# Attention followed by expert routing on one Trainium2 core: moving the token table to the last steps and loading four experts' weights ahead

## The chip, the cores and the metric

The kernel runs on one core of a Trainium2 chip, as one launch. The metric is the device time of the launch in microseconds, taken as the median of several runs. Beside it there is one profiled execution, with its own time, which the trace describes. Engine names in the profile are PE (TensorE matmul), PEld (its weight loads), DVE (VectorE), ACT (ScalarE), POOL (GpSimd) and SP (SyncE). POOL also issues most of the transfers.

## The reference: what is computed

First comes block-causal attention, for 8 batches of 8 heads with 576 positions and head size 64. A position sees all positions of its own 64-wide block and of the blocks before it. The result is laid out as x, 4608 rows (tokens) of 512. Then each row goes through the expert that `moe_domain_id` names for it, one of 8:

```
mask = block_i >= block_j
attn = exp(scores - max); attn = attn / (sum(attn) + 1e-09)
x = (attn @ v).transpose(0, 2, 1, 3).reshape(4608, 512)
for e in range(8):
    out[domain_id == e] = relu(x[domain_id == e] @ w1[e]) @ w2[e]
```

w1[e] is 512 x 1024 and w2[e] is 1024 x 512, both given in float32. The kernel computes in float16 with float32 sums.

## The kernel before

**Attention.** The work is cut into 32 pairs of heads, p = 0 to 31, four per batch. The loop at L445 runs 33 steps, the last of which only drains. In step p the program order is: scores of the first group for pair p (`emit_G(0)`, L323, then the exponential on ACT, L328); the transposes of q and k for pair p+2 (`emit_T`, L311 on PE, copied out of PSUM by DVE at L315); scores of the second group; the products with v for pair p-1 (`emit_P`, L374 and L379); scores of the third group; the rest of p-1 and its normalisation (`emit_Q`, L395 and L396 on DVE); then one piece of the table (L477); then `loads(p)` (L427). The transposes write into PSUM tiles of the tag PT, of which there are two; the table's sums use the same two.

**Loads.** q and k are loaded and cast to float16 on the way by POOL's queue (L69). v comes in float32 into one of three staging tiles `vst` (L78, L82) and is then cast by POOL into `vS` (L110, `cast_v`). Batch b is loaded at step 4b-10, so the last one, b = 7, at step 18, and its v is cast at step 20. In that same `loads(p)` a batch's loads enclose the cast of the batch before. POOL works through its instructions in the order of the program, so casts, table work, load issues and gathers stand in one queue.

**Weights.** An expert's weights are eight pieces, four of w1 (L116) and four of w2 (L119), each of 512 KB in float32 in memory and 256 KB in float16 on the chip. The eight pieces of experts 0 and 1 go into the pool `wsb` (two buffers of each kind), two pieces per step in steps 20 to 27. Experts 2 to 7 use four buffers in the pool `msb`, which is opened after the attention's pool `asb` is closed. Expert 2 is issued after the gathers of experts 0 and 1, expert e+3 during the second product of expert e.

**The table.** `inverse` (L169) turns the rank and domain of each token into a table of row numbers for each expert's 640 slots. It works on four quarters of the columns. For each quarter `differ` makes two differences on POOL (Hq at L184, L at L187), `equal` compares on DVE (L193, L195, L197), `column` multiplies on POOL (L204), and `add` sums with nine matmuls on PE (L213) and one DVE instruction (L217 or L219). Four short DVE instructions (L226 to L234) finish it. It is a generator. One `next` is made at the end of each step from p = 18 on, just before `loads(p)`:

```
for k in range(10):
    for d, f in ((3, add), (2, column), (1, equal), (0, differ)):
        if (k - d) % 2 == 0 and 0 <= k - d < 8:
            f((k - d) // 2)
    yield
```

So a quarter starts every second step, and each of its four stages comes one step after the one before. The first `add` stands at the end of step 21, the last at the end of step 27, and the finish at step 28.

**Between the two halves.** The rows x of a batch are stored to memory as they are done (L412 and L413, on SP's queue, the last part also on ACT's). After the loop 36 matmuls on the identity (L486) run on PE. Then POOL issues the gathers of expert 0 and 1 (L498, five blocks of 128 rows each), which need the table and all the stored rows.

**Experts.** For each expert the first product is `mm1` (L530, then the rectifier on ACT, L536) and the second is `mm2` (L547), whose result DVE copies (L553) and POOL scatters to the output (L554). Between the blocks of `mm2` PE transposes the next expert's rows (L508, copied by DVE at L511). Expert 0 alone does `mm1` in two halves, the first for blocks 0 to 2. A loop at L609 handles experts with more than 640 tokens.

Of the kernel before, what the change touches and what calls it, by code (L numbers as in the profile page):

```python
# [9 lines left out]
F32 = mybir.dt.float32  # L10
F16 = mybir.dt.float16
# [7 lines left out]
def kernel(  # L19
# [11 lines left out]
    B, H, S, D = q.shape  # L31
    N = B * S
    E = moe_w1.shape[0]
# [21 lines left out]

    qh = [asb.tile([128, HP, S], F16, name=f"qh{i}") for i in range(4)]
    kh = [asb.tile([128, HP, S], F16, name=f"kh{i}") for i in range(4)]
    vst = [asb.tile([128, 5, H, D], F32, name=f"vst{i}") for i in range(3)]


    vS = [asb.tile([128, 5, HP, 132], F16, name=f"vS{i}") for i in range(3)]
# [69 lines left out]
    def load_weights(pool, bufs, w1_e, w2_e):  # L131
        w1h, t1 = load_w1(pool, bufs, w1_e)
        w2h, t2 = load_w2(pool, bufs, w2_e)
        return w1h, w2h, t1 + t2


    ones_sq = const.tile([128, 128], F16, name="ones_sq")
    lo_h = const.tile([128, NJ], F16, name="lo_h")
    u_f = const.tile([128, NJ], F32, name="u_f")
# [29 lines left out]
    def inverse(sb, pp, tag, ncols, base, tok):  # L169
        ub = sb.tile([128, NJ], F16, name="ub", tag="ub")  # L170
        nc.vector.tensor_scalar(
            out=ub[:], in0=u_f[:], scalar1=base, scalar2=None, op0=ALU.subtract)
        inv = sb.tile([128, 2, ncols], F32, name="inv", tag="inv")
        fi = inv[:].rearrange("p a c -> p (a c)")
        sh, sl = [128, NQ, ncols], [128, NQ, 128]
        ts = {}

        def differ(qt):
            js = slice(NQ * qt, NQ * qt + NQ)
            L = sb.tile([128, NQ, 128], F16, name="L", tag="L", bufs=2)  # L180
            Hq = sb.tile([128, NQ, ncols], F16, name="Hq", tag="Hq", bufs=2)
            Hh = sb.tile([128, NQ, 2, ncols], F16, name="Hh", tag="Hh", bufs=2)
            ts[qt] = (L, Hq, Hh)
            nc.gpsimd.tensor_tensor(  # L184
                out=Hq[:], in0=iota_h[:, 0:ncols].unsqueeze(1).to_broadcast(sh),
                in1=ub[:, js].unsqueeze(2).to_broadcast(sh), op=ALU.subtract)
            nc.gpsimd.tensor_tensor(  # L187
                out=L[:], in0=iota_h[:].unsqueeze(1).to_broadcast(sl),
                in1=lo_h[:, js].unsqueeze(2).to_broadcast(sl), op=ALU.subtract)

        def equal(qt):
            L, Hq, Hh = ts[qt]
            nc.vector.tensor_scalar(  # L193
                out=Hq[:], in0=Hq[:], scalar1=0.0, scalar2=None, op0=ALU.is_equal)
            nc.vector.tensor_scalar(  # L195
                out=L[:], in0=L[:], scalar1=0.0, scalar2=None, op0=ALU.is_equal)
            nc.vector.tensor_scalar(  # L197
                out=Hh[:, :, 0], in0=Hq[:], scalar1=p_f[:, 0:1], scalar2=None,
                op0=ALU.mult)

        def column(qt):
            L, Hq, Hh = ts[qt]
            js = slice(NQ * qt, NQ * qt + NQ)
            nc.gpsimd.tensor_tensor(  # L204
                out=Hh[:, :, 1], in0=Hq[:],
                in1=iota_h[:, js].unsqueeze(2).to_broadcast(sh), op=ALU.mult)

        def add(qt):
            L, Hq, Hh = ts[qt]
            ps = pp.tile([128, 512], F32, name=tag, tag=tag, bufs=2)  # L210
            pv = ps[:, 0 : 2 * ncols]
            for j in range(NQ):
                nc.tensor.matmul(  # L213
                    out=pv, lhsT=L[:, j], rhs=Hh[:, j].rearrange("p a c -> p (a c)"),
                    start=(j == 0), stop=(j == NQ - 1))
            if qt == 0:
                nc.vector.tensor_copy(out=fi, in_=pv)  # L217
            else:
                nc.vector.tensor_tensor(out=fi, in0=fi, in1=pv, op=ALU.add)  # L219

        for k in range(10):
            for d, f in ((3, add), (2, column), (1, equal), (0, differ)):
                if (k - d) % 2 == 0 and 0 <= k - d < 8:
                    f((k - d) // 2)
            yield
        nc.vector.tensor_tensor(  # L226
            out=inv[:, 0], in0=inv[:, 0], in1=inv[:, 1], op=ALU.add)
        nc.vector.tensor_scalar(
            out=inv[:, 1], in0=inv[:, 0], scalar1=0.0, scalar2=1.0e6,
            op0=ALU.is_equal, op1=ALU.mult)  # L230
        nc.vector.scalar_tensor_tensor(
            out=tok[:, 0], in0=inv[:, 0], scalar=-4.0, in1=inv[:, 1],
            op0=ALU.add, op1=ALU.add)
        nc.vector.tensor_scalar(  # L234
            out=tok[:, 1], in0=tok[:, 0], scalar1=float(N - 1), scalar2=None,
            op0=ALU.min)
        yield
# [189 lines left out]
    def loads(p):  # L427
        fn = nc.gpsimd.tensor_copy
        for b in range(2, B):
            if p == max(0, 4 * b - 10):  # L430
                load_qk(b)
                load_v(nc.gpsimd, b, range(0, 5))
                cast_v(fn, b - 1)
                load_v(nc.gpsimd, b, range(5, H + 1))
        if p == 4 * B - 12:
            cast_v(fn, B - 1)
            for e in range(2):
                w1s[e], w2s[e], t = load_weights(wsb, 2, moe_w1[e], moe_w2[e])
                wts.extend(t)
        for f in wts[:2]:  # L440
            f()
        del wts[:2]

    prev = None
    for p in range(npair + 1):  # L445
        b, hp = divmod(p, HP)
        st = None
        if p < npair:
            st = {"p": p, "QK": QKs.pop(p)}
            if hp == 0:  # L450
                x_t = asb.tile([128, 6, DM], F16, name="x", tag="x", bufs=2)
            st["x"] = x_t
            emit_G(0, st)
        if p and p + 2 < npair:
            QKs[p + 2] = emit_T(p + 2)
        if p < npair:
            emit_G(1, st)
        if prev is not None:
            emit_P(prev)
        if p < npair:  # L460
            emit_G(2, st)
        if prev is not None:
            emit_Q(prev)
            if prev["p"] == npair - 2:
                store_x(prev, 0, DM - 128, nc.sync)
            elif prev["p"] == npair - 1:
                store_x(prev, DM - 128, DM, nc.scalar)
            elif prev["p"] % HP == HP - 1:
                store_x(prev, 0, DM, nc.sync)
        if p == 0:  # L470
            cast_v(nc.scalar.copy, 0)
            QKs[1] = emit_T(1)
            emit_VE(0)
            QKs[2] = emit_T(2)
        if p < npair and hp == 3 and b + 1 < B:
            emit_VE(b + 1)
        if p > 17:  # L477
            next(tabl, None)
        loads(p)
        prev = st  # L480
    for _ in tabl:
# [95 lines left out]
        nc.vector.memset(base_f[:], float(NB * E))  # L577

    xgs = {e: gather(tok_of(e)) for e in range(2)}
    w1s[2], w2s[2], todo = load_weights(msb, 4, moe_w1[2], moe_w2[2])  # L580
    for f in todo:
        f()
    xT = new_xT()
    for e in range(E):
        if e + 2 < E:
            xgs[e + 2] = gather(tok_of(e + 2))
        hT = new_hT()
        if e == 0:
            for i, blks in enumerate(((0, 1, 2), (3, 4))):
                for blk in blks:  # L590
                    transpose_block(xgs[0], xT, blk)
                mm1(xT, hT, w1s[0], (i,))
        else:
            mm1(xT, hT, w1s[e])
        nxt = None
        if e + 1 < E:
            xT = new_xT()
            nxt = (xgs[e + 1], xT)
        todo = ()
        if e + 3 < E:  # L600
            w1s[e + 3], w2s[e + 3], todo = load_weights(
                msb, 4, moe_w1[e + 3], moe_w2[e + 3])
        if e == 1:
            count_rounds()
        mm2(hT, w2s[e], tok_of(e), outs[NB * e : NB * e + NB], todo, nxt)
# [3 lines left out]
    with tc.For_i(0, n_it, 1) as it:  # L609
        e_r = it % E  # L610
        tok = msb.tile([128, 2, NB], I32, name="tok", tag="tok")
        for _ in inverse(msb, mps, "po", NB, base_f[:, 0:1], tok[:]):
            pass
        nc.vector.tensor_scalar(out=base_f[:], in0=base_f[:], scalar1=float(NB),
                                scalar2=None, op0=ALU.add)
        w1h, w2h, todo = load_weights(
            msb, 4, moe_w1[bass.ds(e_r, 1)].rearrange("o d f -> (o d) f"),
            moe_w2[bass.ds(e_r, 1)].rearrange("o d f -> (o d) f"))
        for f in todo:
            f()  # L620
        xg, xT, hT = gather(tok), new_xT(), new_hT()
        for blk in range(NB):
            transpose_block(xg, xT, blk)
        mm1(xT, hT, w1h)
        mm2(hT, w2h, tok, outs[0:NB])
# [30 lines left out]
```

## Time and profile before

| | us |
|---|---|
| median of 9 runs | 333.24 |
| lowest and highest | 330.51 and 336.85 |
| the profiled execution's own time | 336.27 |
| its span, first to last instruction | 334.6 |
| PE busy in the span | 273.9 |
| POOL busy | 220.6 |
| DVE busy | 148.0 |
| ACT busy | 146.3 |
| last PE instruction of the attention, end | 151.5 |
| first matmul of `mm1`, start | 163.3 |

The profile page gives busy times per engine, then the span in 40 slices with a digit for the busy tenths, the clock that TensorE was granted (PEclk) and the share of time in which the 16 DMA engines were busy, and then groups of instructions by line. The trace can be asked for the timeline of an engine, for who waited for whom, and for busy times in any stretch. A wait is written as the line that waited, an arrow and what ended the wait.

### The profile page before, as it was taken

To read this page: it belongs to the slowest core of one execution; us is meant where nothing else is said; L and a number is where in the kernel's file an instruction comes from. 1 tells how busy PE (TensorE), PEld (TensorE's weight loads), DVE (VectorE), ACT (ScalarE), POOL (GpSimd) and SP (SyncE) were. 2 spreads that over 40 slices of the span, in tenths; PEclk is the share of its full clock that TensorE was granted. 3 is DMA by queue.
4 is the path that set the end of the run, shared out by engine and by line. 5 is a ranking of instruction groups with operands and counts; after the bars stand their busy time and mean duration, and the time that the engine had idled before them with its cause. 6 is when DMAs were issued, how large, how long until landed. Compare 5 with 4: busy or idle time off the path is not lost. (4 is left out here: it accounts for less than half of the span.)

```text
span 334.6 us, 8598 instructions
## 1 busy us (share of the span) xinstructions
PE 273.9 (82%) x3658; PEld 177.3 (53%) x3658; DVE 148.0 (44%) x286; ACT 146.3 (44%) x208; POOL 220.6 (66%) x286
## 2 busy tenths in 40 slices
PE   2579887697972889869669999999899899999930
PEld 1357665465751567645335665647466464656510
DVE  3857887376782978651102514040230504042120
ACT  5549787386871568680232240505124060513300
POOL 8669968798899996002786868687786766223230
PEclk9999999597896789799979999999999999999995
DMA  8999999899969399722369998989899695212030
GB/s 161 201 208 200 178 234 202 191 202 227 265 103 265 59 176 211 147 72 80 102 131 246 181 252 170 223 199 216 224 191 235 137 226 174 78 39 104 31 115 1
DMA packets 36537, 55.69 MB, mean 166 GB/s; under 512 B 9902, under 2 KB 22702, under 8 KB 36496
## 3 DMA queue, kind: packets, MB, share of 16 engines
q0 software_dynamic: 26128, 49.17, 69.6%
q1 hardware_dynamic: 9840, 5.81, 6.2%
q8 instruction: 30, 0.49, 0.6%
q10 hardware_dynamic: 528, 0.13, 0.2%
q14 instruction: 11, 0.09, 0.1%
HBM read 67.15 MB, written 15.20 MB: 246 GB/s over the span
## 5 line engine op out<-in xcount | busy, mean ns | idle before, releaser
L328 ACT ACTIVATE A<-ps 128x1024 f16<-128x1024 f32 (+1 forms) x96 | 83.0, 883 | 46.8 <-PE ps L323 31.0
L536 ACT ACTIVATE hT<-ph 128x640 f16<-128x640 f32 (+1 forms) x72 | 46.4, 645 | 117.0 <-PE ph L530 111.2
L547 PE MATMUL po<-w2h,hT 128*128 128x512 f16 x320 | 74.9, 379 | 4.2 <-DVE osb L553 3.6
L530 PE MATMUL ph<-xT,w1h 128*128 128x320 f16 x512 | 73.3, 302 | 3.6 <-DVE xT L511 2.6
L554 POOL DMA_INDIRECT out_dram<-osb,tok x40 | 40.8, 1019 | 44.9 <-DVE osb L553 30.4
L498 POOL DMA_INDIRECT xg<-x_rows,tok x40 | 40.9, 1024 | 37.0 <-issue 36.4
L530 PEld LDWEIGHTS <-w1h 128*128 128x128 f16 x512 | 50.5, 99 | 26.1 <-issue 2.8
L511 DVE COPY xT<-pt 128x512 f16<-128x512 f16 x40 | 16.9, 424 | 105.9 <-PE pt L508 67.5
L78 POOL DMA_DIRECT2D vst<-in_v_dram x56 | 42.8, 796 | 14.0 <-DMA kh<-in_k_dram 7.8
L547 PEld LDWEIGHTS <-hT 128*128 128x128 f16 x320 | 30.1, 98 | 34.3 <-issue 5.0
L315 DVE COPY QK<-PT 128x576 f16<-128x576 f16 x64 | 45.5, 749 | 4.0 <-PE PT L311 3.7
L379 PE MATMUL po<-vS,A 128*128 128x65 f16 x640 | 37.2, 203 | 4.9 <-issue 4.9
L323 PE MATMUL ps<-QK 64*128 64x512 f16 (+3 forms) x256 | 37.8, 335 | 3.9 <-ACT A L328 2.3
L379 PEld LDWEIGHTS <-A 128*128 128x128 f16 x640 | 32.6, 104 | 6.8 <-issue 6.8
L553 DVE COPY osb<-po 128x512 f32<-128x512 f32 x40 | 27.4, 684 | 19.7 <-PE po L547 19.7
L374 PE MATMUL po<-VE,ATE 128*128 128x130 f16 x160 | 33.3, 234 | 2.5 <-DVE x L396 2.5
L396 DVE TENSOR_TENSOR x<-po,rc 128x768 f16<-128x768 f32 x32 | 30.6, 958 | 1.1
L311 PE MATMUL PT<-identh,kh 64*64 64x64 f16 x576 | 17.1, 203 | 8.5 <-DVE inv L219 2.8
L311 PE MATMUL PT<-identh,qh 64*64 64x64 f16 x576 | 17.2, 206 | 5.3 <-DVE QK L315 4.1
L374 PEld LDWEIGHTS <-ATE 128*128 128x128 f16 x160 | 16.0, 100 | 9.8 <-issue 7.5
L311 PEld LDWEIGHTS <-qh 64*64 64x64 f16 x576 | 13.8, 119 | 13.6 <-issue 12.6
L395 DVE RECIPROCAL rc<-po 128x12 f32<-128x12 f32 x32 | 7.4, 232 | 30.2 <-PE po L374 30.2
(85 smaller groups left out, 241.9 us busy)
## 6 DMA issues: line engine op xcount, KB each, us to landing
w1h<-in_moe_w_dram POOLq DMA_DIRECT2D x32, 256.0 KB
w2h<-in_moe_w_dram POOLq DMA_DIRECT2D x32, 256.0 KB
vst<-in_v_dram POOLq DMA_DIRECT2D x63, 128.0 KB
qh<-in_q_dram POOLq DMA_DIRECT2D x14, 288.0 KB
kh<-in_k_dram POOLq DMA_DIRECT2D x14, 288.0 KB
x_rows<-x SPq DMA_DIRECT2D x7, 512.0 KB, 7.8
vst<-in_v_dram SPq DMA_DIRECT2D x9, 128.0 KB, 4.9
xg<-x_rows,tok POOLq DMA_INDIRECT x40
```

The source lines that it names most:

```text
L78: eng.dma_start(out=vst[b % 3][:, 0:4, n], in_=v[b, n, 0:512, :].rearrange("(c p) d -> p c d", p=128))
L311: nc.tensor.transpose(out=PT[h, j], in_=src[h, hp, 64 * j : 64 * j + 64], identity=identh[h, h])
L315: nc.vector.tensor_copy(out=QK[:, s].rearrange("p (n j) -> p n j", j=9), in_=PT[:].rearrange("p j n -> p n j"))
L323: nc.tensor.matmul(out=o[:, i], lhsT=QK[h, 1, 128 * c : 128 * c + 128], rhs=QK[h, 0, 64 + 128 * c : S], start=True, stop=True)
L328: nc.scalar.activation(out=o, in_=i, func=AF.Exp, scale=0.125)
L374: nc.tensor.matmul(out=o[:, 1:131], lhsT=st["AE"][:, 128 * m : 128 * m + 128], rhs=VE[b % 2][:, m, hp, 1:131], start=True, stop=(m == 0))
L379: nc.tensor.matmul(out=o[:, 1 + 65 * i : 66 + 65 * i], lhsT=at_block(st, i, c, m), rhs=vS[b % 3][:, c, hp, 1 + 65 * i : 66 + 65 * i], star ...
L498: nc.gpsimd.indirect_dma_start(out=g[:, blk, :], out_offset=None, in_=xd, in_offset=bass.IndirectOffsetOnAxis(ap=tok[:, 1, blk : blk + 1], ...
L530: nc.tensor.matmul(out=ph[:, i, 0:hw], lhsT=w1_cols(w1h, dc, fc), rhs=xT[:, dc, hw * i : hw * i + hw], start=(dc == 0), stop=(dc == 3))
L536: nc.scalar.activation(out=hT[:, fc].rearrange("p (i n) -> p i n", i=2)[:, i0:i1], in_=ph[:, i0:i1, 0:hw], func=AF.Relu)
L547: nc.tensor.matmul(out=po[:], lhsT=hT[:, fc, 128 * blk : 128 * blk + 128], rhs=w2h[:, fc, :], start=(fc == 0), stop=(fc == 7))
L554: nc.gpsimd.indirect_dma_start(out=dst[blk], out_offset=bass.IndirectOffsetOnAxis(ap=tok[:, 0, blk : blk + 1], axis=0), in_=osb[:], in_off ...
```

## The change

Table: the tiles L, Hq and Hh get four buffers instead of two. A quarter starts every step for four steps, `equal` comes four steps after `differ`, `column` one step later and `add` two steps after that. The calls move from the loop into `loads`, from step 20 to step 31: at step 20 after the cast of the last v, at later steps ahead of that step's two weight pieces.

Weights: `wsb` has three buffers of each kind, used by all experts except 3 and 7. These two lie in the staging tiles of v (w1 in `vst[2]`, w2 in `vst[0]`), which have moved from the attention's pool to `wsb`. At step 20 the 32 pieces of experts 0 to 3 are put in a list, of which two are issued per step from step 21 to step 32; the eight that are left (expert 3) are issued after the gathers of experts 0 and 1. During the second product of expert e, expert e+3 is loaded for e of 1 and more; expert 0's has no loads.

```diff
-    vst = [asb.tile([128, 5, H, D], F32, name=f"vst{i}") for i in range(3)]
+    vst = [wsb.tile([128, 5, H, D], F32, name=f"vst{i}") for i in range(3)]
...
+    def load_vst(w1_e, w2_e):
+        w1h, w2h = (
+            vst[i][:].rearrange("p c h d -> p (c h d)").bitcast(F16)[
+                :, 0 : 8 * DM].rearrange("p (a f) -> p a f", a=a)
+            for i, a in ((2, 4), (0, 8)))
+        return (w1h, w2h, [lambda i=i: w1_piece(w1h, w1_e, i) for i in range(4)]
+                + [lambda i=i: w2_piece(w2h, w2_e, i) for i in range(4)])
+
+    def load_expert(e):
+        if e % 4 == 3:
+            w1s[e], w2s[e], t = load_vst(moe_w1[e], moe_w2[e])
+        else:
+            w1s[e], w2s[e], t = load_weights(wsb, 3, moe_w1[e], moe_w2[e])
+        return t
...
-            L = sb.tile([128, NQ, 128], F16, name="L", tag="L", bufs=2)
-            Hq = sb.tile([128, NQ, ncols], F16, name="Hq", tag="Hq", bufs=2)
-            Hh = sb.tile([128, NQ, 2, ncols], F16, name="Hh", tag="Hh", bufs=2)
+            L = sb.tile([128, NQ, 128], F16, name="L", tag="L", bufs=4)
+            Hq = sb.tile([128, NQ, ncols], F16, name="Hq", tag="Hq", bufs=4)
+            Hh = sb.tile([128, NQ, 2, ncols], F16, name="Hh", tag="Hh", bufs=4)
...
-        for k in range(10):
-            for d, f in ((3, add), (2, column), (1, equal), (0, differ)):
-                if (k - d) % 2 == 0 and 0 <= k - d < 8:
-                    f((k - d) // 2)
+        for k in range(11):
+            for d, f in ((7, add), (5, column), (4, equal), (0, differ)):
+                if 0 <= k - d < 4:
+                    f(k - d)
...
         if p == 4 * B - 12:
             cast_v(fn, B - 1)
-            for e in range(2):
-                w1s[e], w2s[e], t = load_weights(wsb, 2, moe_w1[e], moe_w2[e])
-                wts.extend(t)
-        for f in wts[:2]:
-            f()
-        del wts[:2]
+            next(tabl)
+            for e in range(4):
+                wts.extend(load_expert(e))
+        if p > 4 * B - 12:
+            next(tabl, None)
+            for f in wts[:2]:
+                f()
+            del wts[:2]
...
-        if p > 17:
-            next(tabl, None)
         loads(p)
...
     xgs = {e: gather(tok_of(e)) for e in range(2)}
-    w1s[2], w2s[2], todo = load_weights(msb, 4, moe_w1[2], moe_w2[2])
-    for f in todo:
+    for f in wts:
         f()
...
         todo = ()
-        if e + 3 < E:
-            w1s[e + 3], w2s[e + 3], todo = load_weights(
-                msb, 4, moe_w1[e + 3], moe_w2[e + 3])
+        if e and e + 3 < E:
+            todo = load_expert(e + 3)
```

The loop for experts with more than 640 tokens takes its weights from `wsb` with three buffers instead of from `msb` with four.

More of the change, by code (lines that the diff above doesn't have):

```diff
@@ L616 @@
         w1h, w2h, todo = load_weights(
-            msb, 4, moe_w1[bass.ds(e_r, 1)].rearrange("o d f -> (o d) f"),
+            wsb, 3, moe_w1[bass.ds(e_r, 1)].rearrange("o d f -> (o d) f"),
             moe_w2[bass.ds(e_r, 1)].rearrange("o d f -> (o d) f"))
```

## The prediction

> **What bounds the kernel now.** I read the page's slices first, then the busy times by stretch, then who waited, and last the timelines of the engines from 86 to 182 us. Of the slices the fourth row is the share of the DMA engines:
>
> ```profile
> PE   2579887697972889869669999999899899999930
> ...
> PEclk9999999597896789799979999999999999999995
> DMA  8999999899969399722369998989899695212030
> ```
>
> PE is full from 178 us (slice 21) on, and TensorE's clock is full there. The DMA engines are full up to 140 us and nearly idle from 140 to 170 us. By stretch (columns: PE, PEld, DVE, ACT, POOL busy, clock, DMA share, GB/s):
>
> ```profile
> 98.00:152.00 54.00, 40.06 (x881) 29.51 (x881) 37.21 (x67) 32.34 (x45) 31.76 (x41) 0.84 0.75 153
> 152.00:178.00 26.00, 20.09 (x118) 11.08 (x117) 2.83 (x6) 6.42 (x15) 17.40 (x21) 0.93 0.52 117
> 178.00:322.00 144.00, 138.88 (x910) 83.10 (x907) 41.14 (x85) 39.98 (x58) 89.83 (x107) 1.00 0.73 171
> ```
>
> From 178 us the experts are bound by PE, 139 of 144 us, and the change removes no matmul. So what it can win lies between 98 and 178 us. Two things stand there. First, the table in the attention's last steps. The waits of PE from 98 to 152 us:
>
> ```profile
> PE PT L213 <- POOL Hh L204: 6.5, 1, 6.5
> PE PT L311 <- DVE inv L219: 2.8, 3, 1.4
> ```
>
> The first sum of step 21 waits 6.5 us for `column`, which POOL reaches only behind step 18's loads and cast. Then DVE's first comparison after it takes 3.87 us where its fellows take 0.25, and the clock is 0.53 from 104 to 114 us. Steps 21 to 24 take from 97.3 to 124.05 us (starts of the first score group), 26.7 us for four, where steps 25 and 27 take 3.3 us each.
>
> Second, the passage to the experts. PE's timeline:
>
> ```profile
> 163.32 4.67 PE L530 MATMUL ph<-xT,w1h 128*128 128x320 f16 x28 [0.52 <-DVE xT L511]
> ...
> 171.97 6.22 PE L530 MATMUL ph<-xT,w1h 128*128 128x320 f16 x32 [2.09 <-DVE xT L511]
> ...
> 178.25 1.89 PE L547 MATMUL po<-w2h,hT 128*128 128x512 f16 x8
> ```
>
> PE's last attention matmul ends at 151.5, the last row store is issued at 152.8, POOL's first gather comes at 156.8, `mm1` starts at 163.3 and `mm2` of expert 0 at 178.25. So `mm1` of expert 0 takes 14.9 us; of the later experts it takes 8.9. The gathers come 1.31 us apart and its second half waits for blocks 3 and 4.
>
> **What the Trainium skill says.** "SBUF — State Buffer", Who interferes with whom: a VectorE copy, cast or tensor_scalar in a two-port mode and a GpSimd instruction exclude each other, and the later one waits for the whole of the other. The trace agrees: the comparison of 3.87 us (109.2 to 113.1) lies under POOL's L187 (108.9 to 111.0) and cast (110.9 to 113.5). "TensorE: Matmul & The Clock Gate", Part 1: after an idle window of about 3.4 us the clock is halved, and it comes back after about as long of work. The trace agrees: 0.50 from 104 to 112 us after PE's idle 101.75 to 108.2. "DMA: Bandwidth & Descriptors", SWDGE vs HWDGE vs iDMA: of GpSimd's transfers only one queue is allocated. So gathers would stand behind weights issued before them; in the kernel before the queue was empty at the first gather, so no row shows it there. The same page, Issuing engines are not separate DMA queues: SP's stores share the 16 engines with that queue. The trace agrees: the 512 KB row store took 8.0 us to land from 95 to 110 us, the last ones 2.5 to 4.1 in idle.
>
> **The change part by part.**
>
> *Loads of batch 7.* In the kernel before, POOL waits 1.67 us at 90.3 for DVE's `ub` and spends 2.9 us (L184 0.79, L187 2.10) on step 18's differences, then starts the loads at 94.8. These steps leave POOL's queue there, so the loads start at 90.3. The transfers of batch 6 end near 92.8; batch 7 with a row store took 13.1 us (96.1 to 109.2), so v lands near 106, not 109.
>
> *POOL's chain.* v's cast takes 2.6 us: 108.6. Then per step one `differ` (2.9) and, from step 21, two pieces (1.1): differ 0 to 3 end at 111.5, 114.4, 118.4 and 122.4. Pieces of steps 23 and 24: 124.6. Column 0 (0.85): 125.5. Each next step adds 2.0: the last column at 131.5, and the last ten pieces (0.56 each) at 137.1.
>
> *PE's steps.* With 3.0 us each (87.44 to 90.44, steps 18 and 19) PE ends step 24 near 110 and comes upon equal 0, which needs differ 0: DVE stops there, behind it the copies of q and k, behind these PE. So PE falls into POOL's stride until the first sum, at the end of step 27, can have column 0: 126.0. The 6.5 us wait thus does not vanish wholly; part is now spread over steps 25 to 27. Afterwards: step 28 at 3.3 plus the PT wait behind DVE's batch copy (1.4) plus a sum (0.45); step 29 at 3.35 plus 0.4 plus 0.45; step 30 at 3.0 plus 0.45; step 31 and the drain 5.4 as before (146.1 to 151.5). That is 18.2 and gives the attention's end at 144.2, 7.3 us earlier. DVE's work is the same count: four times 1.1 us, now in four adjacent steps with 2.6 us of other work, 3.7 in all, within POOL's stride of 4.
>
> *The exclusion.* Not shown for this placing. Differ 1 to 3 run on POOL while equal 0 to 2 come due. At best it costs nothing; at worst four comparisons each wait out an L187, 4 x 2.1 = 8.4 us. I take nothing, since the next comparison must wait for that same differ anyway, so POOL's end covers it; without this cover all of it comes to the path.
>
> *Weights.* In the kernel before, 16 pieces and a row store took 25.3 us (114.5 to 139.8); less 1.8 for the store that is 1.47 us a piece. Now 24 pieces go ahead of the gathers. The first start at 115.2, two per 4 us; from 123 the queue is never empty. Twenty pieces at 1.47 are 29.4, two row stores 3.6: the queue is clear at 156. The piece's price has bounds: all of the bytes at the 211 GB/s of 132 to 138 us gives 262/211 = 1.24 us; charging the whole DMA time of the experts, 0.73 x 144, to the 48 pieces there gives 2.2. I take 1.47, since it is of the same pieces in the same stage.
>
> *The passage.* Rows: end 144.2, store 1.3, landing 4 (idle) to 8 (loaded): gathers begin at 149.5 to 153.5, and a block is there 3.4 us later, 153 to 157. The weights' end at 156 is thus the later or equal one; expert 2's weights, which used to come after the gathers, now stand before them. By then POOL has described several blocks, so they land together: `mm1` near 158, and its halves run on without the gap. But the 36 matmuls end at 152, so PE idles 6 us and starts at half clock: 8.9 + 2.0. `mm2` of expert 0 starts at 168.9, against 178.25: **9.3 us**.
>
> *Experts.* Eight pieces leave `mm2` of expert 0 (8 x 0.57 = 4.6 us of POOL, hidden beside PE). Expert 3's take expert 2's old place after gather 1, and are needed some 45 us later. The loads during experts 1 to 4 are the same, so I count none of the 0.5 to 1.7 us waits there as gained. Changed tile places cost nothing that I can see: the old readers are done long before.
>
> Sum: -9.3 us. The profiled span would be 325.3 and its time 327.0 where it was 336.3; the profiled execution was 3.0 us above the median, in nothing that the change touches as far as one profile tells, so I subtract from the median: 333.2 - 9.3 = 323.9, or **324**.
>
> **Rivals.**
> *The exclusion and cold clock cost half their bound* (4 us): attention ends at 148.2, the stores are then under the weights' end, gathers at 155.5 to 157.5, `mm1` at 161.5, warm after 2 us: 172. Time 327. For it: the 3.87 us. Against: only one of four showed it.
> *The weights do not hold the gathers*, at 1.24 us a piece: queue clear at 151.4; then `mm1` is the attention's end plus 11.8 as before, 156, with hardly a gap, or less if the end is earlier too: 318 to 321.
> *The wait only moves*: everything won is given to the queue, clear at 164 to 168. Time 332 to 336.
> *Slower*: the queue drains so slowly that the gathers come later than before. `mm2` starts at the queue's end plus 12.9; this passes 178.25 when the end is at 165.4, that is at (165.4 - 122.9 - 3.6)/20 = 1.94 us a piece. At 2.2 it clears at 170.5, `mm2` starts at 183.4, and the time is 338. For it: stores, gathers and weights share the engines. Against: 1.47 measured.
> That the change does not do what it says: were the new buffers made to wait for old readers, the pieces of steps 29 to 32 would come after the attention as now; the table alone would then win up to its 7.3 us: 326 to 328. No old reader is due there.
>
> **How the numbers follow.** Likeliest, with its own range 319 to 327: 0.55. Exclusion: 0.15. Weights not holding: 0.10. New buffers waiting: 0.03. The wait moves: 0.10. Slower: 0.07. The range of 315 to 331 leaves out the last and most of the one before it, and some below for an attention that ends earlier than my chain of POOL allows. One per cent, about what a measurement can tell here, is 3.3 us: faster is under 329.9, which the first four give, 0.83; same 0.10; slower 0.07.
>
> **What would show it.** Right: no 6.5 us wait at L213 in step 21; loads of batch 7 starting at POOL near 90 us; PE or DVE waiting for L184 or L187 in steps 24 to 27 instead; the attention's last matmul near 144; DMA full from 123 to 156; the first gathered block landing with the last weights and not 3.4 us after its issue; `mm1` of expert 0 in one run of about 11 us, half of it slow. Wrong: L193 at 2 us and more several times; DMA idle before the first gather; a gap between the halves of `mm1`; PE waits for weights in the experts, which I count at none.

## The result, and the profile after

| | before | after |
|---|---|---|
| median, us | 333.24 (31 runs) | 342.81 (10 runs, 338.14 to 345.5) |
| ratio after to before | | 1.0266, 95% interval 1.0222 to 1.031 |
| the profiled execution's own time, and its span | 336.27, 334.6 | 347.0, 345.2 |
| last attention matmul, end | 151.54 | 152.58 (predicted 144.2) |
| first gather | 156.81 | 161.31 |
| first matmul of `mm1`, expert 0 | 163.32 | 168.03 (predicted 158) |
| first matmul of `mm2`, expert 0 | 178.25 | 181.36 (predicted 168.9) |
| first product of expert 1, from its first matmul to the first of the second product | 8.92 | 16.70 |

The kernel became slower where a gain was forecast. The ratio compares only those executions of each kernel that lie within 1.5% of its fastest; by that measure both profiled ones are slow. The profiled execution of the kernel after is longer than all ten of the median, so its waits need not be those of a usual execution; the experiments below say which of them come again. The line numbers of the kernel after are some 16 higher than those shown above. Its slices first (PE, clock, DMA engines):

```profile
PE   2589888869878067985789679989999898999940
...
PEclk9999899996999659899699969999999999999995
...
DMA  8999999999990589993379413989979895202030
```

A slice is 8.6 us, counted from 0. Of the clock's dips, two matter here: the one in slices 13 and 14 (112 to 129 us) and, new, the one in slice 23 (198 to 207 us), among the experts, where the kernel before was full. The DMA row reads 9 in slices 15 to 17 (129 to 155 us), where it read 9, 7 and 2: weights now fill the end of the attention. In exchange it reads 1 in slice 23. By stretch, cut again at the attention's end and at the start of expert 0's `mm2` (PE, PEld, DVE, ACT, POOL busy, clock, DMA share, GB/s):

```profile
98.00:152.60 54.60, 37.08 (x867) 27.51 (x862) 44.82 (x65) 30.97 (x43) 34.30 (x45) 0.84 0.79 158
152.60:181.40 28.80, 21.62 (x125) 12.06 (x124) 3.22 (x7) 6.62 (x16) 16.72 (x20) 0.88 0.56 126
181.40:322.00 140.60, 131.66 (x861) 79.24 (x859) 37.46 (x80) 38.34 (x56) 81.79 (x95) 0.98 0.65 155
```

Neither of the first two stretches is shorter than before. DVE is 7.6 us busier in the first although its instructions are no more, and PE has lost 9 of 140.6 us in the third, where before it lost 5 of 144. Three places account for it.

**First, DVE is kept out by POOL.** The waits of PE from 98 to 153 us no longer hold the 6.5 us for `column`. In its place:

```profile
PE PT L327 <- DVE QK L331: 12.7, 1, 12.7
```

DVE's timeline at that point, with `emit_VE` of batch 6 (L421, two copies together), and POOL's in the same time:

```profile
107.87 0.96 DVE L412 TENSOR_TENSOR x<-po,rc 128x768 f16<-128x768 f32 x1
108.74 13.96 DVE L421 COPY VE<-vS 64x1280 f16<-64x1280 f16 x2
122.74 1.42 DVE L331 COPY QK<-PT 128x576 f16<-128x576 f16 x2
```

```profile
105.74 2.58 POOL L110 CAST vS<-vst 128x1024 f16<-128x1024 f32 x3 [3.45 <-PE PT L327]
108.29 0.79 POOL L200 TENSOR_TENSOR Hq<-iota_h,ub 128x360 f16<-128x360 f16 x1
109.04 2.10 POOL L203 TENSOR_TENSOR L<-iota_h,lo_h 128x1152 f16<-128x1152 f16 x1
...
113.91 1.14 POOL L116 DMA_DIRECT2D w1h<-in_moe_w_dram  x2
115.05 0.82 POOL L200 TENSOR_TENSOR Hq<-iota_h,ub 128x360 f16<-128x360 f16 x1
...
119.72 2.13 POOL L203 TENSOR_TENSOR L<-iota_h,lo_h 128x1152 f16<-128x1152 f16 x1
121.77 2.18 POOL L119 DMA_DIRECT2D w2h<-in_moe_w_dram  x4
```

The copies begin 0.3 us ahead of POOL's first long difference (109.04); the first of them takes 13.46 us and ends 0.35 us after the last difference (121.85), the second takes 0.49. It waited not for one POOL instruction but for the whole row, and the weight issues inside the row (1.14 us at 113.91) did not let it in. The copies of q and k stand behind it on DVE, and PE behind these.

The wait comes again in other executions, but its length depends on when DVE arrives. Five of the kernels below have the same attention as this one (they differ from it only behind the attention): there the waiting instruction took 7.9 to 11.6 us and the attention ended at 149.0 to 153.2. In all traces together, eleven DVE instructions waited over 5 us for this row, and ten of them ended 0.12 to 0.36 us after its last difference. The eleventh, in the table half alone, got in one long difference earlier.

**Second, the last row store lands late.** The line that gives the landing times of the row stores, for the kernel before and then for the one after; the smallest is the last store's, which in the kernel before met idle DMA engines:

```profile
DMA to landing us min/median/max: 2.7/7.1/10.4
```

```profile
DMA to landing us min/median/max: 6.1/9.5/13.7
```

The last store was issued at 153.88, while weight pieces kept the engines full to about 158 us; the first gather follows its landing by 1.3 us in both kernels (156.81 and 161.31).

**Third, the first product of expert 1 stalls**, by 7.8 us. In the kernel before, PE ran it in one piece, and POOL issued weight pieces between the scatters:

```profile
187.77 8.86 PE L530 MATMUL ph<-xT,w1h 128*128 128x320 f16 x64
```

```profile
185.36 1.04 POOL L554 DMA_INDIRECT out_dram<-osb,tok  x1 [0.31 <-DVE osb L553]
186.39 1.09 POOL L116 DMA_DIRECT2D w1h<-in_moe_w_dram  x2
187.78 1.04 POOL L554 DMA_INDIRECT out_dram<-osb,tok  x1 [0.30 <-DMA w1h<-in_moe_w_dram]
188.81 1.10 POOL L119 DMA_DIRECT2D w2h<-in_moe_w_dram  x2
```

In the kernel after, PE's timeline, ACT's, and POOL's around it:

```profile
190.89 3.42 PE L546 MATMUL ph<-xT,w1h 128*128 128x320 f16 x24
194.59 1.25 PE L546 MATMUL ph<-xT,w1h 128*128 128x320 f16 x8 [0.28 <-ACT hT L552]
198.84 1.39 PE L546 MATMUL ph<-xT,w1h 128*128 128x320 f16 x8 [3.01 <-issue]
201.71 5.82 PE L546 MATMUL ph<-xT,w1h 128*128 128x320 f16 x24 [1.48 <-ACT hT L552]
```

```profile
193.83 0.70 ACT L552 ACTIVATE hT<-ph 128x640 f16<-128x640 f32 x1 [0.95 <-PE ph L546]
198.09 0.70 ACT L552 ACTIVATE hT<-ph 128x640 f16<-128x640 f32 x1 [3.55 <-remote]
```

```profile
192.06 0.99 POOL L570 DMA_INDIRECT out_dram<-osb,tok  x1 [0.30 <-DVE rie L257]
193.35 1.05 POOL L514 DMA_INDIRECT xg<-x_rows,tok  x1 [0.30 <-issue]
194.70 1.02 POOL L514 DMA_INDIRECT xg<-x_rows,tok  x1 [0.30 <-issue]
```

PE's third group of matmuls stands in the records as ended at 194.31, but its signal to ACT comes at 198.06, 3.75 us late; the next one's comes 5.1 us late. ACT waits, PE has no free accumulator, idles, and goes on at half clock (0.50 from 200 to 206 us). In that time POOL does nothing but issue: five gathers, five scatters, five gathers from 178.97 to 199.63, mostly 1.3 us apart. Expert 3's weight pieces no longer stand between these scatters. A late load of instructions does not show as the reason: among the DMA transfers from 186 to 208 us none is one of an instruction queue.

The budget of the profiled executions, after less before: attention's end +1.0, first gather a further +3.5, `mm2` of expert 0 -1.4 (the gap inside its `mm1` is shorter), expert 1's first product +7.8, the rest -0.3; together 10.6, the difference of the spans.

### The profile page after: what moved, and what is told of

The parts are those of the page before. It is cut to its first block, busy times and chain, and to the rows that moved or that the text cites. A ratio compares the mean times of both kernels' runs of the same rounds, so it can differ in the third digit from the quotient of the medians.

```text
span 345.2 us, 8603 instructions
## 1 busy us (share of the span) xinstructions
PE 275.7 (80%) x3658; PEld 177.7 (51%) x3658; DVE 156.9 (45%) x286; ACT 145.9 (42%) x208; POOL 220.6 (64%) x286
## 5 line engine op out<-in xcount | busy, mean ns | idle before, releaser
L527 DVE COPY xT<-pt 128x512 f16<-128x512 f16 x40 | 16.9, 424 | 116.5 <-PE pt L524 99.1
L546 PE MATMUL ph<-xT,w1h 128*128 128x320 f16 x384 | 59.1, 315 | 6.3 <-issue 3.0
L563 PE MATMUL po<-w2h,hT 128*128 128x512 f16 x240 | 56.7, 379 | 3.4 <-DVE osb L569 3.4
L514 POOL DMA_INDIRECT xg<-x_rows,tok x40 | 40.8, 1019 | 28.8 <-PE ps L502 16.5
L546 PEld LDWEIGHTS <-w1h 128*128 128x128 f16 x384 | 39.3, 103 | 25.9 <-issue 6.7
L327 PE MATMUL PT<-identh,qh 64*64 64x64 f16 x576 | 17.4, 206 | 16.9 <-DVE QK L331 14.4
L421 DVE COPY VE<-vS 64x1280 f16<-64x1280 f16 x16 | 21.1, 1318 | 1.3 <-ACT vS L110 0.9
```

The costliest lines, as they stand in the source:

```text
L327: nc.tensor.transpose(out=PT[h, j], in_=src[h, hp, 64 * j : 64 * j + 64], identity=identh[h, h])
L514: nc.gpsimd.indirect_dma_start(out=g[:, blk, :], out_offset=None, in_=xd, in_offset=bass.IndirectOffsetOnAxis(ap=tok[:, 1, blk : blk + 1], ...
L546: nc.tensor.matmul(out=ph[:, i, 0:hw], lhsT=w1_cols(w1h, dc, fc), rhs=xT[:, dc, hw * i : hw * i + hw], start=(dc == 0), stop=(dc == 3))
L563: nc.tensor.matmul(out=po[:], lhsT=hT[:, fc, 128 * blk : 128 * blk + 128], rhs=w2h[:, fc, :], start=(fc == 0), stop=(fc == 7))
```

## The experiments

**The two halves apart.** Table half alone (four buffers, the new `table` order and its calls in `loads`; weights as before):

```diff
-        for k in range(10):
+        for k in range(11):
...
-        if p > 17:
-            next(tabl, None)
```

> The table half alone: the table's new place and spacing with four buffers, and the weights as in the kernel before (two experts ahead, in their own pool). Theory L (lockout): the copy of v's first rows by VectorE in step 23 (VE<-vS) cannot start while GpSimd has casts and differences queued one after the other[...], and that wait of some 12 us eats all that the table's new place wins. Then this kernel has a VE copy of 8 us or more, the attention ends within 3 us of 151, and the time is 331 to 336, no gain over before. Rival Q (queue): the loss is that of the weights ahead of the gathers, and the table half by itself wins its 7 us: 325 to 328.

Measured: 333.52 us, ratio 1.0054 (1.0025 to 1.0083), in theory L's range. The copy of batch 6 took 11.5 us, at 107.55, and the attention ended at 149.5, so that 2 us of the predicted 7.3 were left there. Its trace also showed something that no theory had: expert 6's first product took 14.9 us, 6.0 more than in the kernel before. The time of the whole is thus not that of the table alone.

Weights half alone (four experts ahead, the old table):

> The weights half alone: four experts ahead, the fourth in v's landing tiles, with the table as before (steps 18 to 28, one step between stages, two buffers). Theory L: no VE copy over 1 us, the attention ends near 151; the last row stores land 3 us later under the weights' transfers, so the gathers start 3 to 4 us later and the first product of expert 0 starts on half the clock; 335 to 339. Rival Q: the whole loss is here, 341 to 344.

Measured: 339.44, ratio 1.0226 (1.0139 to 1.0314). The time was 0.4 us over theory L's range, and its reason held only in part: the first gather came at 161.44, 8.6 us behind the attention, but the larger loss was expert 1's first product, 16.85 us, which the expectation did not have. (The profiled execution, 347.06, was the longest of the four.)

**Is it the row on POOL that keeps DVE out?** The changed kernel with the copy of batch 6 two steps earlier:

```diff
-        if p < npair and hp == 3 and b + 1 < B:
+        if p < npair and hp == (1 if b == 5 else 3) and b + 1 < B:
             emit_VE(b + 1)
```

> The changed kernel, with the copy VE<-vS of batch 6 in step 21 instead of 23, ahead of the queue of casts and differences on GpSimd. Theory L: the copies take 0.5 us each, and the wait moves to the next VectorE instruction[...], the comparison of the first quarter in step 24 (L209), which takes 5 to 10 us; the attention ends 3 to 5 us earlier than in the changed kernel; 337 to 340. Rival S: the copy waited for something of its own (the cast of batch 6, a buffer), and nothing like it comes up at the comparison: 330 to 333, or, if it waits as long in step 21, 343.

Measured: 341.24, ratio 1.0321 (1.0237 to 1.0405). The place behaved as the theory has it. The copy went through, and the next instruction of the kind to meet the row, the first comparison, waited instead, for 5.63 us where its fellows take 0.25:

```profile
113.14 5.63 DVE L209 TENSOR_SCALAR Hq<-Hq 128x360 f16<-128x360 f16 x1
118.69 0.45 DVE L211 TENSOR_SCALAR L<-L 128x1152 f16<-128x1152 f16 x1
```

The attention ended at 146.06, 6.5 us earlier, more than the expected 3 to 5. The first gather was 8.0 us behind the attention instead of 8.7, and expert 1's first product still took 16.64 us. The median hardly moved, and the expected 337 to 340 was missed by 1 us, though the profiled execution (339.64) was 7.4 us shorter than that of the kernel after: as said, the latter was a long one.

The changed kernel with the stages of a quarter one step apart (3, 2, 1, 0 instead of 7, 5, 4, 0):

> The changed kernel with one step between the stages of the table (differences, comparison, product, sum), still one quarter per step from step 20 on. The product on GpSimd waits for the comparison on VectorE and so breaks GpSimd's queue after the second pair of differences. Theory L: with the queue broken VectorE gets in there; no VectorE instruction waits longer than some 6 us, the attention ends 3 to 6 us earlier than in the changed kernel; 336 to 340. Rival P (plain lateness): short distances only make TensorE wait for the product as in the kernel before, so the time stays or grows: 343 to 347.

Measured: 342.82, ratio 1.0335 (1.025 to 1.042), attention's end 154.63. The gain in the attention did not come, and the time was 0.2 us short of rival P's range: the comparisons now met the row (4.96 and 1.73 us for two of them) and the columns stood in POOL's queue between the differences. The broken row did shorten the longest wait, to less than the 6 us that theory L had. Expert 1's first product took 14.46.

**What stalls expert 1's first product?** The theory by now was that the unbroken row of gathers and scatters does, which the change made by taking expert 3's pieces out of expert 0's second product. Undone alone in the changed kernel, and made alone in the kernel before:

```diff
-    for f in wts:
+    for f in wts[:-8]:
         f()
...
-        todo = ()
+        todo = () if e else wts[-8:]
```

> The changed kernel with one thing undone: expert 3's eight weight pieces are issued two behind each scatter of expert 0's second product, as in the kernel before, and not right behind the first ten gathers. Theory I (an unbroken row of gathers and scatters on POOL that overlaps a first product makes PE's semaphore increments late; weight pieces in the row prevent it): expert 1's first product takes 8.9 to 9.5 us instead of 16.7, nothing else moves, and the time is 334 to 338. Rival J (the stall comes from where the weights lie or from the quiet time of the DMA engines earlier on): expert 1's first product stays above 14 us and the time at 341 to 345.

Measured: 343.31, ratio 1.0329 (1.0235 to 1.0424). The time was the rival's, the trace neither's: expert 1's first product was back at 8.92, but expert 0's took 21.78 instead of 13.33. With the pieces gone from behind the gathers of experts 0 and 1, those ten and the five of expert 2 made a new row of fifteen, from 156.2 to 175.6, and the stall went with the row:

```profile
171.39 0.61 PE L524 MATMUL pt<-identh,xg 128*128 128x128 f16 x8
177.96 6.75 PE L546 MATMUL ph<-xT,w1h 128*128 128x320 f16 x32 [5.96 <-DVE xT L527]
```

The transposes recorded from 171.39 on signalled DVE at 176.04, 0.45 us after the row's end.

> The kernel before with one thing of the change in it: expert 3's eight pieces are issued behind the first ten gathers, right after expert 2's, so that expert 0's second product has none. Theory I: expert 1's first product grows from 8.9 to 14 to 17 us, and the time from 333 to 338 to 342. Rival J: it stays at 8.9 and the time at 331 to 335. A third outcome is open: POOL issues eight pieces more ahead of the gathers of expert 2, so the gathers come some 8 us later, and the stall could move to a later product.

Measured: 343.57, ratio 1.0332 (1.024 to 1.0423). Theory I's outcome, with a time 1.6 us over its range: expert 1's first product took 16.61, beside a row of fifteen from 185.4 to 205.0. This one move in the kernel before costs as much as the whole change.

**Do the late stores come from the pieces ahead of them?** As the run with expert 3's pieces in the second product, and no pieces in the last three steps of the attention:

```diff
-            for f in wts[:2]:
+            for f in wts[: 2 if p < 30 else 0]:
                 f()
-            del wts[:2]
+            del wts[: 2 if p < 30 else 0]
```

> As the run with expert 3's pieces in expert 0's second product, and beside it no weight piece is issued in the last three steps of the attention; the six left over follow the first ten gathers, as expert 2's did before. Theory C (the last row store lands 6 us after its issue instead of 2.7 because pieces stand ahead of it in the DMA engines): the first gather starts 4 to 5 us after the last attention matmul instead of 8.7, and the time is 3 to 5 us under that of the run beside it, 330 to 334. Rival K (the store is slow for another reason): 8 to 9 us and no gain.

Measured: 335.81, ratio 1.0103 (1.0023 to 1.0182). The last store landed in 2.7 us and the first gather came 4.0 us behind its issue, 5.3 behind the last attention matmul (before: 4.0 and 5.3; after: 7.4 and 8.7). For the store that is theory C, 0.3 us outside the expected figure. The six pieces left over broke the first row, so no first product stalled. The time is 1.8 us over the expected range, and 7.5 below the run beside it; but that run's first product of expert 0 was 8.1 us longer, so what the earlier store is worth in time is not separated here. DVE's wait is still there: a comparison took 12.85 us at 112.1. That it is all that is left over the kernel before is not shown.

**All three at once.** The last run's edits, with the copy of batch 6 in step 21 and `equal`, `column` and `add` one step later:

> Three changes on the changed kernel at once: the VE copy of batch 6 moved from step 23 to step 21 and the comparisons one step later (so that no DVE instruction that PE needs stands behind POOL's unbroken table work), no weight piece in the last three steps, and expert 3's pieces in expert 0's second product. If theories L, C and I are all right: the attention ends at 144 to 147, the first gather starts at 148 to 151, expert 1's first product takes 8.9, and the time is 324 to 329, faster than the kernel before. If one of the three falls, it is 331 to 336.

Measured: 328.28 us, in the range for all three, ratio 0.9896 (0.9863 to 0.9928). In its profiled execution, at 341.81 the longest of its 21 runs, the copy in step 21 met POOL's row after all, and the attention ended at 158.5:

```profile
110.76 12.66 DVE L421 COPY VE<-vS 64x1280 f16<-64x1280 f16 x2
```

Probably the copy comes first in the shorter executions, but no trace shows one of them. To have it ahead of the row in any case, it went to step 20 (`hp == (0 if b == 5 else 3)`):

> As the run with the three changes together, with the VE copy of batch 6 in step 20 instead of 21, ahead of the cast that opens POOL's unbroken table work. In the profile of that run the copy in step 21 still began 1.7 us behind the first difference and took 12.16 us. Theory L: in step 20 it ends before the cast of batch 7 begins, takes under 1 us a half, the attention ends at 143 to 147, the first gather starts 4 to 5 us later, and the time is 324 to 328 with less spread. Rival Q2 (the attention's end is set by something else in these steps): it ends at 149 or later and the time is 329 to 333.

Measured: 327.52, ratio 0.9897 (0.976 to 1.0035, few runs of the kernel before). The attention's end and the time were in theory L's ranges. The first gather came 6.1 us behind the attention, where 4 to 5 were expected: the last store took 3.5 us to land. The same kernel again, with more runs of the kernel before:

> The same kernel as the run with the VE copy in step 20, again, in five rounds. If the three repaired causes are what held the change back: 326 to 329 us and a ratio to the kernel before of 0.98 to 0.99 with its interval under 1. If that run's median of four was luck: 330 to 334 and an interval that holds 1.

Measured: 331.58 where the kernel before took 337.21 on that chip, ratio 0.978 (0.9679 to 0.988). The time is in the second range, but the chip was slower for both kernels; the interval holds no 1, as the first had it. In its profile a comparison still waited 6.2 us, and the attention ended at 144.1. DVE's timeline of the former, with the copies of batches 5 and 6, and then its busy times by stretch:

```profile
97.39 0.97 DVE L421 COPY VE<-vS 64x1280 f16<-64x1280 f16 x2
...
100.86 0.98 DVE L421 COPY VE<-vS 64x1280 f16<-64x1280 f16 x2
101.86 0.24 DVE L187 TENSOR_SCALAR ub<-u_f,base_f 128x36 f16<-128x36 f32 x1
```

```profile
90.00:143.20 53.20, 47.67 (x1117) 35.19 (x1113) 40.80 (x76) 40.52 (x56) 35.36 (x44) 0.89 0.85 175
143.20:169.50 26.30, 21.73 (x125) 12.08 (x124) 3.90 (x11) 6.54 (x16) 16.49 (x19) 0.87 0.48 113
169.50:313.00 143.50, 138.75 (x906) 82.84 (x903) 40.71 (x85) 39.74 (x57) 89.11 (x106) 1.00 0.70 168
```

Both copies take under 1 us, the attention ends at 143.2, `mm2` of expert 0 starts at 169.4, and in the experts PE is busy 138.75 of 143.5 us, as in the kernel before. Its span is 326.5.

**What in the row does it: its pieces' traffic, their issue, or any work?** Three additions to the changed kernel, eight each, two behind each of the first four scatters of expert 0's second product; what they load or set is read by nobody. Small loads by POOL:

```diff
+            t = msb.tile([128, 8], F16, name=f"probe{j}")
+            nc.gpsimd.dma_start(out=t[:], in_=moe_w1[3][0:128, 0:8])
```

> The changed kernel with eight small casting loads of 4 KB each (128 rows of 8 numbers, read by nobody) issued by POOL two behind each scatter of expert 0's second product; everything else stays. Theory I2 (what counts is that the row of gathers and scatters on POOL is broken by direct loads, whatever their size): expert 1's first product takes under 10 us instead of 16.7 and the time is 334 to 338. Theory I3 (what counts is the weights' traffic): it stays at 14 to 17 us and the time at 341 to 345.

Measured: 337.4, ratio 1.0243 (1.0135 to 1.0351); expert 1's first product 8.91. Memsets by POOL (`nc.gpsimd.memset` of 128 x 512):

> The changed kernel with eight POOL memsets of 128 by 512 numbers (of tiles that nobody reads) two behind each scatter of expert 0's second product, in place of loads. Theory I1 (any work of POOL between the gathers and scatters breaks the row and slows it): expert 1's first product takes under 10 us and the time is 334 to 338. Theories I2 and I3: 14 to 17 us and 341 to 345.

Measured: 338.01, ratio 1.0231 (0.9965 to 1.0497); expert 1's first product 8.91. POOL's timeline there, and PE's in the same time:

```profile
184.71 1.01 POOL L570 DMA_INDIRECT out_dram<-osb,tok  x1 [0.38 <-issue]
185.71 1.01 POOL L616 MEMSET probe<- 128x512 f32 x2
186.89 0.99 POOL L570 DMA_INDIRECT out_dram<-osb,tok  x1 [0.17 <-DVE osb L569]
```

```profile
187.38 8.86 PE L546 MATMUL ph<-xT,w1h 128*128 128x320 f16 x64
```

The traffic alone, by SP (`nc.sync.dma_start` of 512 KB each, behind a small DVE memset):

> The changed kernel with the traffic of expert 3's eight pieces alone: eight loads of 512 KB without a cast, issued by SP behind a small DVE memset, two behind each scatter of expert 0's second product, into tiles that nobody reads; POOL's row of gathers and scatters stays unbroken. Theory I3 (the weights' traffic beside the row keeps PE's increments in time): expert 1's first product takes under 10 us and the time is 334 to 338. Theories I1 and I2: 14 to 17 us and 341 to 346.

Measured: 344.23, ratio 1.0437 (1.035 to 1.0525); expert 1's first product 16.90, with 320 GB/s moving beside it. In these three the kernel before itself ran from 329.07 to 337.07, so they are better compared with each other: the two that mend the product are 6 to 7 us shorter than the one that does not. So traffic on SP's queue neither causes the stall nor cures it, and both kinds of small POOL work put between the scatters cure it, as the weight pieces do in the kernel before. Only the first two of the memsets:

> The changed kernel with only the first two of the eight POOL memsets, behind the first scatter of expert 0's second product, so that the row of 15 falls into 6 and 9. Theory R (the length of the row counts, with a bound of about 8 to 10): expert 1's first product takes 9 to 12 us and the time is 335 to 340. Rival S (each scatter needs room behind it, or the place of the last gathers counts): it takes 14 to 17 us and the time is 341 to 345.

Measured: 345.01 where the kernel before took 337.21 on that chip, ratio 1.0286 (1.0221 to 1.0352); expert 1's first product 11.94. That is theory R's figure, though not its time, which is 5 us over its range; 4 us of that are the chip's, by the kernel before. In its profiled execution the copy's wait for the row was 11.3 us.

Over the traces, this is what products of experts 1 to 7 took beside rows of gathers and scatters on POOL. A row is counted in POOL's timeline, as far as no other POOL work stands in it; a pause is a time of over 0.5 us in it in which POOL waits. A row that begins only in the second half of a product is left out.

| row | pauses in it | first product, us | where |
|---|---|---|---|
| up to 7 | none to 2.4 us | 8.7 to 9.2 | experts other than 6, pieces or memsets between the scatters |
| 9 | one of 0.9 us | 11.9 | expert 1, one pair of memsets |
| 15 | none to 1.4 us | 14.5 to 16.9 | expert 1: after, weights half, copy early, short spacing, pieces taken out of the kernel before, SP loads |
| 11 | 1.0 us behind the tenth | 14.9 | expert 6, table half alone |
| 11 | 2.6 us behind the ninth | 10.7 | expert 6, small loads |
| 11 | 0.8 to 2.4 us from the sixth or seventh on, and more | 8.9 | expert 6, the fourteen other traces |

At one and the same place, expert 1 of the changed kernel with its last five gathers beside the product, a row of 6 (all memsets) gives 8.9, of 9 (one pair) 11.9, of 15 (none) 16.7. Expert 6 has no weight pieces beside it in any kernel, and its row of 11 stalls PE only where nine or ten follow each other without a pause:

```profile
278.38 2.20 PE L531 MATMUL ph<-xT,w1h 128*128 128x320 f16 x15 [0.36 <-DVE xT L512]
284.49 8.08 PE L531 MATMUL ph<-xT,w1h 128*128 128x320 f16 x48 [3.91 <-ACT hT L537]
```

(the table half alone). So pauses seem to count too. They do not decide it alone: with the copy early, the row of 15 has one of 1.4 us behind the sixth, and the product still took 16.6. Memsets put both work and 1 us of time between two scatters; whether the work or the time cures the stall, the runs do not tell apart.

## Why the prediction was wrong, point by point

*"I take nothing" for the exclusion.* This step failed. The bound was put on the four comparisons and capped at 8.4 us, one instruction of POOL each. The Trainium skill's page "SBUF — State Buffer", Who interferes with whom, has the lock held for a whole instruction, and says that copies take part; the trace agrees, and goes further: the loser waited for eight POOL instructions in a row and the issues between them, 13.46 us in one copy. The prediction also took the wrong instruction: what met the row first was `emit_VE` of batch 6 in step 23, which it does not name; the four comparisons that it feared took 0.24 us each. With that copy ahead of the row and the comparisons a step later the attention ended at 143.2 (144.1 in the second profile), against the predicted 144.2. The account of POOL's chain stood as far as the differences: loads of batch 7 at 89.85 (predicted 90.3), differences ending at 121.85 (122.4). The columns, which wait for the comparisons, then came late, the last at 138.3 (131.5).

*The passage.* The queue ran empty near 158 (predicted 156), but the weights' end did not cover the store. The last store landed in 6.1 us instead of 2.7, inside the predicted 4 to 8, and from an attention's end at 152.6 that came to 160, behind the weights. The prediction also had `mm1` in one run of 10.9 us; it took 13.3, with a gap between its halves. Predicted from the attention's end to `mm2`: 24.7 us. After: 28.8. Of the 4.1 us, 1.7 lie ahead of `mm1` and 2.4 in it. Two of the named signs of being wrong were there: idle DMA engines before the first gather (158 to 161 us) and the gap.

*"hidden beside PE" for the eight pieces of expert 0's second product.* This step failed too: expert 1's first product took 7.8 us longer. Taking eight issues out of POOL's queue was held to be free because POOL had time there. POOL had; but without them its gathers and scatters close up to a row of fifteen, and PE's signals come late beside such a row.

*The sum.* Of the 20 us between the predicted span (325.3) and the measured one (345.2), 8.4 are the attention, 4.1 the passage and 7.4 the experts. With the copy in step 20 and the other repairs, the profiled span was 326.5, and `mm2` of expert 0 began at 169.4 (predicted 168.9). That is one execution, and of a kernel in which comparisons and pieces have moved too. The ratios put the gain at 1.0 to 2.2 per cent, by estimate 3.5 to 7.4 us (of the kernel before's 333 and 337), where 9.3 were forecast. So part of the forecast gain was there, perhaps most of it; the change as made lost it and ended 2.7 per cent above the kernel before. The rivals: the slower one had the right side by the wrong mechanism (pieces at 2.2 us, 338); the one with half the exclusion's bound had the right mechanism at half its size.

*Left open.* Why PE's signals come late is not settled. The ends of matmuls in the records are modelled, so the trace does not tell a signal held back from matmuls that ran late. That it depends on POOL's row, and not on the traffic of SP's loads, the place of the weights or the expert, is shown; what the two engines share is not, nor how long a row must be and what pause ends it. In the first product of expert 0, which has ten gathers beside it in most kernels, it was not told apart from the ordinary wait for blocks.

## What to carry to other kernels

Work packed on GpSimd without gaps has a cost on the engines beside it that its own busy time does not show: ask for every VectorE copy or tensor_scalar issued while the row runs what stands behind it, and price it at the rest of the row, not at one instruction. Issues taken out of a queue are not free to remove if they were what kept gathers and scatters apart. Loads pulled ahead compete with the last store that a dependent stage waits for, so stop them a few steps before it.

## What the runs showed of the hardware that was not expected

- Beside rows of 9 to 15 gathers and scatters on GpSimd, mostly 1.3 us apart, TensorE's signals came up to 5.1 us late and a product of 8.9 us took 10.7 to 16.9. Rows of up to 7, and rows of 11 in which GpSimd paused for 0.8 to 2.4 us from the sixth or seventh on, did nothing. Two memsets of 0.55 us or two loads of 4 KB behind each of four scatters removed it; 4 MB of loads by SP did not.
- The exclusion between VectorE and GpSimd lasted over a row of up to eight GpSimd tensor instructions with weight issues between: 13.46 us for a copy of 0.5 us. Of eleven waits of over 5 us, ten ended 0.12 to 0.36 us after the row's last instruction of that kind. With the same attention, VectorE's copy was the one that waited in five profiled executions; in a sixth the copy got through beside GpSimd's casts, and a comparison waited 11.6 us in its place.
